# Two FNet and two H3 layers in one kernel: branch loads issued by GpSimd, row statistics on ScalarE, another rotation of PSUM banks

## The chip, the cores and the metric

The kernel runs on one core of a Trainium2 chip. The metric is the device time of one execution in microseconds (us); lower is better. The engines are TensorE (PE: matmuls; PEld: its weight loads), VectorE (DVE), ScalarE (ACT), GpSimd (POOL) and SyncE (SP). ACT, POOL and SP also issue DMAs, each from its own queue, in the order in which its instructions stand.

## The reference

The input x has 2048 rows and 576 columns. Four sublayers are applied, each to the layer norm of what came before, and added to it:

```python
x = x + A(layernorm(x))      # layer 1, Fourier mixing
x = x + B(layernorm(x))      # gated long convolution
x = x + A(layernorm(x))      # layer 2
x = x + B(layernorm(x))
# A(n) = Cr @ (n @ Wr.T) - Ci @ (n @ Wi.T), Cr, Ci: 2048 x 2048, Wr, Wi: 576 x 576
# B(n) = n * y, y = causal_conv(kv, ssm_k) + kv * ssm_D, kv = shift_conv(k) * v
```

`A` is a DFT over the rows and one over the columns, of which the real part is kept. In `B`, k, v and ssm_k are inputs, so that y depends on no layer: it is computed once (here by transforms in place of the FFT) and used by both `B` sublayers as a gate.

## The kernel before

**Numbers.** Products are made at fp32 accuracy from pairs: `split` (L77) writes the rounded high part on ACT (L78) and the rest on DVE (L79), and each product is three matmuls, high by high, high by low, low by high. Rows are held interleaved, 128 partitions of 16 rows j; x[:, j, :] is a tile of 128 x 576.

**Layer 1.** `layer` (L271) runs 128 steps: 4 blocks tb of 512 output rows, in each 2 matrices g (cosine, sine) of 16 steps k. A step loads one 128 x 512 tile of c_mat (`load_c`, L185; SP's queue), splits it, and issues 14 matmuls of 512 columns into four accumulators s0 to s3 and a bank rm. When a block's g is done, `evac_u` (L235) and `evac_r` empty the banks. The product with W (`hidden`, L247) follows in pieces of 27 matmuls of 288 columns that `finish` (L262) puts between the steps. Its result is row xa, stored in DRAM.

**The branch.** `branch` (L316) is a generator that computes y; the loop at L560 advances it along with the steps of layer 1. First transform, up to step 40: for each j, rows of ssm_k and of v with its shifts of k are loaded (`f1_loads`, L343), combined and split on DVE and ACT (`f1_split`, L358), multiplied by f1c, and written to DRAM as t (L387). Middle pass, steps 43 to 96: 64 groups; `mid_split` (L410) loads 288 KB of t (mid<-t) into a ring of three buffers and splits it, `mid_forward` (L417) transforms it, multiplies the spectra of k and v (ACT L424 to L427, DVE L430 to L433), `mid_inverse` (L438) transforms back and stores (copy L444, DMA L445). Last transform, steps 97 to 112: `i2_split` (L464) loads two tiles of 288 KB for each j (mid<-vd) and i2c, `i2_products` (L474) stores y as yb. f1c and i2c are loaded from POOL's queue (`load_fr`, L140), all other loads of the branch from SP's; stores go from ACT's queue.

**Rows of layer 2.** From step 113 on, `get_x1(m)` (L531) makes row m: it loads xa, `gated` (L493) adds the first `B` sublayer, `normed` (L159) normalises for layer 2, and `to_x` (L165) splits into X. `norm_stats` (L149) takes mean and variance on DVE (bn_stats L153 for each half of a row, bn_aggr L154, eps L155) and the reciprocal root on POOL (L156); `normed` scales on ACT (L162) after a small DVE operation (L161). A second function, `normed_x` (L501), serves half of layer 1's rows: sums and squares are taken on ACT with accumulated outputs (L504, L506), small operations on DVE (L505, L507, L509), the power on POOL (L508), the scaling on ACT (L510).

**Layer 2.** Its block 0 runs as 32 ordinary steps. At the same time normalised rows come back from DRAM (`build_load`, L598) and `build` (L607) makes the sums and differences of X ("X's sums") that the next blocks need: from step B_FROM = 18 on, two of the four parts of a `build` in each step, a new `build` every second step. After steps 15 and 31 the accumulators are emptied by `save_u` (L644: ACT L646, then a store) and `store_r` (L649: ACT L652, DVE L653). Blocks 1 to 3 are computed by `strassen` (L720): seven products m in the order 5, 1, 6, 2, 7, 3, 4, each of four steps kp. `load_step` (L668) loads c_mat by 512 KB and sums it on DVE (L671, L677). Each product goes into a pair of banks, s0 and s1 or s2 and s3. Products 2 and 4 accumulate onto products 1 and 7 and use their banks; every other product takes `pair()` (L72), which alternates by a counter at each call. So 5, 1, 6, 7 and 3 take pairs in turn, 2 has 1's and 4 has 7's. After a product ACT or DVE empties its banks (L755 to L780; 2's is ACT L762, 4's DVE L776 and `store_r`). The last stage is `hidden` for all four blocks, with the second `B` sublayer.

**Order.** A scheduler orders each engine's instructions ahead of time from the order in which the program issues them; each engine then runs its own list in order and waits for semaphores. `tc.issue_after` puts an instruction behind a named other one.

The lines that the change and the prediction's steps touch are these; line numbers are those of the profile of the kernel before.

Of the kernel before, what the change touches and what calls it, by code (L numbers as in the profile page):

```python
# [10 lines left out]
F32 = mybir.dt.float32  # L11
# [6 lines left out]
D = 576  # L18
# [23 lines left out]
STAT = 20  # L42
STATIC = 14
B_LOAD = 15
B_FROM = 18
X_RING = 8
CSB = 5
X_END = J * 2 * D
RT_AT = 8 + 4 * STAT
# [5 lines left out]
def fnet_h3_kernel(ctx: ExitStack, tc: tile.TileContext, x, c_mat, w_re, w_im, k_pad, v, shift_k,  # L55
                   ssm_k, ssm_d, f1c, i2c, midc, out):
    nc = tc.nc
# [9 lines left out]
        return psp.tile([P, NT], F32, tag="b", bufs=3, name="bk")  # L67

    acc4 = [psp.tile([P, NT], F32, tag=f"s{i}", name=f"s{i}") for i in range(4)]
    pairs = [0]  # L70

    def pair():  # L72
        pairs[0] += 1
        at = pairs[0] % 2 * 2
        return acc4[at:at + 2]

    def split(h, l, src):  # L77
        nc.scalar.activation(h, src, AF.Copy)  # L78
# [12 lines left out]
    def region_b(dt, name):  # L91
        return sb.tile([P, 6 * WIDE], dt, tag="rb", name=name)
# [9 lines left out]
    ring = {}  # L102
# [28 lines left out]
    lay(flts, 8, ("stat", STAT, 4), ("rt", NT, 1))  # L131
    lay(mats, X_END, ("cs", WIDE, 3))

    anchor, stored, pows = [], [], []

    def load_after(dst, src):
        with tc.issue_after(anchor[-1]):
            return nc.sync.dma_start(dst, src).ins

    def load_fr(dst, src):  # L140
        if pows:
# [17 lines left out]
    def normed(src, y):  # L159
        mv, rs, nb = norm_stats(src)  # L160
        nc.vector.tensor_scalar(nb, mv[:, 0:1], rs, -1.0, op0=OP.mult, op1=OP.mult)  # L161
        nc.scalar.activation(y, src, AF.Identity, bias=nb, scale=rs)  # L162
        return y
# [9 lines left out]
    t_d = [dr.tile([P, J, 2, 2, HD], F32, name=f"t{h}") for h in range(2)]  # L173
# [11 lines left out]
    def load_c(step):  # L185
        g, tb, k = step
        raw = ring["craw"]()
        anchor.append(load_after(raw, c_mat[g, tb, k]) if anchor else nc.sync.dma_start(raw, c_mat[g, tb, k]).ins)
        c = ring["cs"]()
        t = c[:, :NT], c[:, NT:]  # L190
        split(t[0], t[1], raw)
        CT[step] = t
# [123 lines left out]
    def branch():  # L316
# [15 lines left out]

        def load_k(i):
            t = two(ring["k"]())
            nc.sync.dma_start(t, bass.AP(tensor=k_pad.tensor, offset=k_pad.offset + 2 * i * D,
                                         ap=[[J * D, P], [1, 2 * D]]))
            for n in range(2):
                kr[2 * i + n] = t[:, n, :]
# [4 lines left out]
        def f1_loads(j, src):  # L343
            if fcs[0] != j:
                fc = quads(ring["fc"]())
                load_fr(fc, f1c[j])
                fcs[:] = j, fc
            r = ring["land" if src else "v"]()
            nc.sync.dma_start(r, (ssm_k if src else v)[:, j, :])
            if not src:  # L350
                if not wt:
                    load_w4()
                while loaded[0] < min((J + 4) // 2, 2 + j, j // 2 + KR):
                    load_k(loaded[0])
                    loaded[0] += 1
            return r, fcs[1]
# [52 lines left out]

        def mid_split(hf, qg):  # L410
            df = parts("df")
            nc.sync.dma_start(df[1].bitcast(F32),
                              t_d[hf][4 * qg:4 * qg + 4].rearrange("q j c s d -> (q j c) (s d)"))
            split_in(*df)
            return df

# [47 lines left out]
        def i2_split(j):  # L464
            fc = quads(ring["fc"]())
            load_fr(fc, i2c[j])
            vf = []
            for c in range(2):
                vf.append(parts("vf"))
                nc.sync.dma_start(vf[c][1].bitcast(F32), v_d[:, j, c])  # L470
                split_in(*vf[c])
            return fc, vf

# [41 lines left out]
    def load_x(j):  # L515
        if j < J:
            XL[j] = ring["x"]()
            nc.sync.dma_start(XL[j], x[:, j, :])
# [12 lines left out]
    def get_x1(j):  # L531
        if j in ready:
            return
        ready.add(j)
        xa = ring["xa"]()
        nc.sync.dma_start(xa, xa_d[j])
        xb = gated(xa, j)
        nc.sync.dma_start(xb_d[j], xb)
        y = normed(xb, xa)
        stored.append(nc.sync.dma_start(y_d[j // 2][:, j % 2, :], y).ins)  # L540
        X[j] = to_x(y, j)

# [5 lines left out]
    br = branch()  # L548
    wl = load_w()
    load_x(0)  # L550
    load_x(1)
    for used in range(1, K_FIRST + 1):
        next(br)
        if used <= 2:
            load_c((0, 0, used - 1))
        if used == PRE:
            get_x0(0)
        if used == PRE + 1:
            get_x0(1)
    for n in layer(get_x0, lambda j: x[:, j, :], done0, pending):  # L560
        if n <= F1_END:
            want = K_FIRST + (F1_16 * n // 16 if n <= 16 else F1_16 + (32 - K_FIRST - F1_16) * (n - 16) // (F1_END - 16))
        elif n <= MID_END:
            want = 33 + 64 * max(0, n - W_END) // (MID_END - W_END)
        else:
            want = min(114, 97 + 17 * (n - MID_END) // (I2_END - MID_END))
        while used < want:
            next(br, None)
            used += 1
        if F1_END < n <= W_END:  # L570
            for _ in range(3):
                next(wl, 0)
        if n >= W_SAVE and n % 2 == 0:
            next(wl, 0)
        if n > W_END:
            finish(pending, 1)
        m = n - PREP
        if m == 0:
            lay(flts, SC_AT + 3 * NT + 2 * D, ("xa", D, 2), ("yb", D, 2))
            lay(region_b(F32, "gate"), 0, ("xa", D, 3), ("yb", D, 3))  # L580
        if 0 <= m < TB * (TB - 1):
            get_x1(m)
    T, R, t7 = {}, {}, []
# [136 lines left out]
    def strassen():  # L720
        acc, rem = {}, {}
        for n, (tb, m, kp) in enumerate(steps):
            if kp == 0:
                if m in (2, 4):
                    acc[m] = acc[1 if m == 2 else 7]
                else:
                    acc[m] = pair()
                if m in (5, 1):
                    g = REMS[m][0]
                    rem[g] = psp.tile([P, NT], F32, tag="rm", name="rm") if g else bank()  # L730
            for i in range(2):
                ahead(n + 4, 2 * n + i + CSB)
                c = cs.pop(2 * n + i)
                first, last, more = kp == 0 and i == 0, kp == KP - 1 and i == 1, m in (2, 4)
                ch, cl = c[:, 0], c[:, 1]
                for d in range(2):
                    ps = acc[m][d]
                    xh, xl = left(m, kp, i, d)
                    mm(ps, xh, ch, first and not more, False, more)
                    mm(ps, xh, cl, False, False, more)  # L740
                    mm(ps, xl, ch, False, last, more)
                if m in REMS:
                    ps, xr = rem[REMS[m][0]], left_r(m, kp, i)
                    mm(ps, xr, ch, first and not more, False)
                    mm(ps, xr, cl, False, last and more)
            if kp == KP - 1:
                if m == 5:
                    m5 = post("both")
                    for i in range(2):
                        nc.scalar.activation(m5[:, i, :], acc[5][i], AF.Copy)  # L750
                elif m == 1:
                    u2 = post("both")
                    for i in range(2):
                        nc.scalar.activation(u2[:, i, :], acc[1][i], AF.Copy)
                elif m == 6:  # L755
                    for i in range(2):
                        nc.vector.tensor_tensor(u2[:, i, :], u2[:, i, :], acc[6][i], OP.add)
                    nc.vector.tensor_tensor(m5, m5, u2, OP.add)
                elif m == 2:
                    t = post()  # L760
                    for i in range(2):
                        nc.scalar.activation(t[:, i, :], acc[2][i], AF.Copy)  # L762
                    store_u(tb, 0, 0, t)
                    store_r(tb, 0, rem[0])
                elif m == 7:
                    t = post()
                    for i in range(2):
                        nc.vector.tensor_tensor(t[:, i, :], m5[:, i, :], acc[7][i], OP.add)
                    store_u(tb, 1, 1, t)
                elif m == 3:  # L770
                    for i in range(2):
                        nc.vector.tensor_tensor(m5[:, i, :], m5[:, i, :], acc[3][i], OP.add)
                    store_u(tb, 0, 1, m5)
                else:
                    for i in range(2):
                        nc.vector.tensor_tensor(u2[:, i, :], u2[:, i, :], acc[4][i], OP.add)  # L776
                    store_u(tb, 1, 0, u2)
                    store_r(tb, 1, rem[1])
            yield tb, m, kp
# [122 lines left out]
```

## Time and profile before

| what | value |
|---|---|
| median of 3 runs | 1257.11 us (1254.49 to 1259.69) |
| profiled execution | 1256.88 us |
| its span (first to last instruction) | 1254.0 us |
| granted TensorE clock | 0.997 |
| matmuls | 6320 |
| DMA moved | 258.28 MB, mean 206 GB/s |

A page of the profile has the busy time of each engine, the chain of work that ended last, the costliest groups of instructions (line, engine, operation, output and inputs by their names in the program, shape, count; then busy time and mean duration in ns; then the idle time of the engine just before them, with what ended it), and the DMAs by line with the time from issue to landing. Other views of the same trace give the waits of an engine ("PE bk L64 <- ACT f1r L78: 9.8, 1, 9.8": matmuls into bk waited for ACT at L78, in all 9.8 us, once, at most 9.8 us), busy times in stretches of the span, and the instructions in order of time. "bk" are three rotating PSUM banks, "s" the four accumulators, "mats" X and the split c_mat. Idle time of an engine that is not the bottleneck costs nothing.

The stages in the trace: head to about 60 us; first transform of the branch beside layer 1 to about 210; loading of W to 260; middle pass 260 to 570; last transform 570 to 655; rows of layer 2 from 655; layer 2's block 0 ends at about 848; Strassen blocks to 1133; last products with W to 1254.

### The profile page before, as it was taken

How to read it: one execution, taken by the hardware profiler on the slowest of the kernel's cores; microseconds unless marked ns; L12 is line 12 of the kernel's file. 1: busy time of each engine (PE TensorE's matmuls, PEld its weight loads, DVE VectorE, ACT ScalarE, POOL GpSimd, SP SyncE). 2: the span in 40 equal slices, each digit the busy share in tenths (PEclk: the TensorE clock that was granted, in tenths of full speed). 3: DMA queues.
4: the chain of work that ended last, by engine and by line, in shares of the span. 5: the costliest groups of instructions: out<-in, count | busy, mean ns of one | idle time of the engine just before them, and what ended most of it. 6: DMA issues, size and time to landing. Idle time of an engine off the chain costs nothing.

```text
span 1254.0 us, 18238 instructions
## 1 busy us (share of the span) xinstructions
PE 1193.0 (95%) x6320; PEld 1027.0 (82%) x6320; DVE 860.0 (69%) x1591; ACT 631.9 (50%) x1250; POOL 73.8 (6%) x102
## 2 busy tenths in 40 slices
PE   6999999999999999999998899999999999999997
PEld 5788887988789877788886698788778777879997
DVE  7999894478865788863359954765666667675674
ACT  6865665277855788753453422534344344450210
POOL 2210000000000000000013210000000000000111
PEclk9999999999999999999999999999999999999999
DMA  9979887446645645547898844763574577777631
GB/s 311 321 251 296 275 259 229 143 137 181 202 153 178 180 141 161 158 122 241 257 292 279 266 148 162 250 229 106 142 269 135 144 247 249 243 268 224 208 136 48
DMA packets 141646, 258.28 MB, mean 206 GB/s; under 512 B 15345, under 2 KB 39921, under 8 KB 141554
## 3 DMA queue, kind: packets, MB, share of 16 engines
q1 hardware_dynamic: 102674, 205.73, 52.0%
q10 hardware_dynamic: 33984, 42.48, 9.7%
q0 software_dynamic: 4896, 8.92, 2.7%
q8 instruction: 49, 0.80, 0.3%
q14 instruction: 43, 0.35, 0.1%
HBM read 190.42 MB, written 66.65 MB: 205 GB/s over the span
## 4 chain that ended last, share of the span: by engine, by line
PE 68%; DMA 10%; DVE 9%; ACT 8%; issue 3%; POOL 1%; ACTq 0%; SPq 0%; POOLq 0%; DVEq 0%
PE s L64 35%; PE bk L64 27%; PE rm L64 6%; DMA ph<-in_c_mat 3%; DMA flts<-in_c_mat 2%; DVE mats L79 2%; DMA t<-flts 1%; DVE flts L153 1%; POOL flts L156 1%; ACT mats L78 1%; ACT mid L78 1%; DMA mid<-t 1%; ACT flts L444 1%; DVE ph L677 1%; ACT flts L425 1%
## 5 line engine op out<-in xcount | busy, mean ns | idle before, releaser
L64 PE MATMUL s<-mats 128*128 128x512 f32 x2094 | 525.8, 392 | 14.3 <-DVE mats L79 7.9
L64 PEld LDWEIGHTS s<-mats 128*128 128x128 f32 x2094 | 384.6, 188 | 91.6 <-DVE mats L79 10.8
L78 ACT ACTIVATE mats<-flts 128x512 fp32r<-128x512 f32 x209 | 130.8, 626 | 148.2 <-PE rm L64 100.0
L79 DVE TENSOR_TENSOR mats<-flts,mats 128x512 fp32r<-128x512 f32 x209 | 142.6, 684 | 58.6 <-ACT mats L78 58.1
L64 PEld LDWEIGHTS bk<-mid 128*128 128x128 f32 x768 | 111.5, 188 | 34.7 <-ACT flts L444 13.6
L64 PE MATMUL bk<-mid 128*128 128x288 f32 x768 | 127.5, 302 | 12.6 <-ACT flts L444 7.6
L64 PE MATMUL bk<-w,u 128*128 128x288 f32 x864 | 123.0, 296 | 3.2 <-ACT w L78 1.2
L64 PEld LDWEIGHTS bk<-w,u 128*128 128x128 f32 x864 | 118.0, 188 | 7.1 <-ACT w L78 1.6
L79 DVE TENSOR_TENSOR mid<-mid 128x576 fp32r<-128x576 f32 x96 | 72.4, 756 | 57.2 <-ACT mid L78 52.2
L64 PE MATMUL rm<-mats 128*128 128x512 f32 x338 | 105.7, 390 | 1.5 <-DVE flts L432 1.2
L78 ACT ACTIVATE mid<-mid 128x576 fp32r<-128x576 f32 x96 | 65.5, 683 | 72.0 <-DMA mid<-vd 41.7
L156 POOL TENSOR_TENSOR flts<-flts 128x1 f32<-128x1 f32 x56 | 46.8, 837 | 579.7 <-DVE flts L155 576.4
L64 PEld LDWEIGHTS rm<-mats 128*128 128x128 f32 x338 | 63.2, 188 | 15.1 <-DVE flts L432 1.4
L64 PE MATMUL bk<-f1r 128*128 128x288 f32 x384 | 61.7, 305 | 13.8 <-ACT f1r L78 9.8
L64 PEld LDWEIGHTS bk<-f1r 128*128 128x128 f32 x384 | 57.6, 195 | 18.7 <-ACT f1r L78 9.8
L64 PE MATMUL s<-t,mats 128*128 128x512 f32 x258 | 64.4, 389 | 0.0
L386 ACT ACTIVATE flts<-bk 128x288 f32<-128x288 f32 x128 | 47.9, 408 | 24.2 <-DMA t<-flts 13.7
L64 PEld LDWEIGHTS s<-t,mats 128*128 128x128 f32 x258 | 48.7, 189 | 10.2
L64 PE MATMUL bk<-mats 128*128 128x288 f32 (+1 forms) x340 | 56.7, 309 | 0.0
L64 PE MATMUL s<-mats,u 128*128 128x512 f32 x198 | 50.3, 389 | 1.9 <-DVE ph L776 1.9
L78 ACT ACTIVATE mats<-ph 128x512 fp32r<-128x512 f32 x45 | 27.8, 629 | 45.5 <-DVE ph L677 17.5
L64 PEld LDWEIGHTS bk<-mats 128*128 128x128 f32 x340 | 48.8, 188 | 2.0
(141 smaller groups left out, 1553.1 us busy)
## 6 DMA issues: line engine op xcount, KB each, us to landing
flts<-in_c_mat SPq DMA_DIRECT2D x150, 256.0 KB, 3.5
ph<-in_c_mat SPq DMA_DIRECT2D x48, 512.0 KB, 4.1
t<-flts ACTq DMA_DIRECT2D x64, 288.0 KB, 4.5
mid<-t SPq DMA_DIRECT2D x64, 288.0 KB, 3.0
flts<-in_c_mat SPq DMA_DIRECT2D x36, 512.0 KB, 5.1
vd<-flts ACTq DMA_DIRECT2D x64, 144.0 KB, 3.0
mid<-vd SPq DMA_DIRECT2D x32, 288.0 KB, 4.3
ud<-ph ACTq DMA_DIRECT2D x12, 512.0 KB, 5.4
```

What stands on the lines that cost most here:

```text
L64: nc.tensor.matmul(ps, lhsT, rhs, start=first, stop=last, skip_group_check=more)
L78: nc.scalar.activation(h, src, AF.Copy)
L79: nc.vector.tensor_tensor(l, src, h.bitcast(F32), OP.subtract)
L153: nc.vector.bn_stats(st[:, i, :], src[:, i * HD:(i + 1) * HD])
L156: pows.append(nc.gpsimd.tensor_tensor(rs, ve, mhalf, OP.pow).ins)
L386: nc.scalar.activation(so[:, c, :], ps[:, :HD], AF.Copy)
L425: nc.scalar.activation(kk[hi, 0, :], pk[lo, :HD], AF.Copy)
L444: nc.scalar.activation(vo, pv[:, :HD], AF.Copy)
L677: nc.vector.tensor_tensor(src, src, r, OP.add)
```

## The change

Six edits:

- From step 15 of layer 1 on (BULK_FROM), the branch's loads of k, ssm_k, v, t and vd are issued by GpSimd (`load_bulk`), each behind the last POOL power issued; before that step by SyncE, as they were.
- `get_x1` calls `normed_x` in place of `normed`, with buffers of their own ("xj") for the discarded output.
- The rings "xa" and "yb" in the gate region have four buffers in place of three.
- `pair` remembers the last pair used, the shared pair of products 2 and 4 included, and returns the other one. So 7 no longer takes 2's pair, and the next block's 5 no longer 4's.
- B_FROM is 20 in place of 18: X's sums begin two steps of layer 2 later.
- The second load of x is issued after the branch's first step in place of before it.

```diff
-B_FROM = 18
+B_FROM = 20
+BULK_FROM = 15
...
-    pairs = [0]
-    def pair():
-        pairs[0] += 1
-        at = pairs[0] % 2 * 2
-        return acc4[at:at + 2]
+    last_pair = [acc4[2:]]
+    def pair(m, acc):
+        if m in (2, 4):
+            last_pair[0] = acc[1 if m == 2 else 7]
+        else:
+            last_pair[0] = acc4[2:] if last_pair[0][0] is acc4[0] else acc4[:2]
+        return last_pair[0]
...
+    def load_bulk(dst, src):
+        if step[0] < BULK_FROM:
+            nc.sync.dma_start(dst, src)
+        else:
+            with tc.issue_after(pows[-1]):
+                nc.gpsimd.dma_start(dst, src)
...
-            nc.sync.dma_start(t, bass.AP(tensor=k_pad.tensor, ...
+            load_bulk(t, bass.AP(tensor=k_pad.tensor, ...
-            nc.sync.dma_start(r, (ssm_k if src else v)[:, j, :])
+            load_bulk(r, (ssm_k if src else v)[:, j, :])
-            nc.sync.dma_start(df[1].bitcast(F32), t_d[hf]...
+            load_bulk(df[1].bitcast(F32), t_d[hf]...
-                nc.sync.dma_start(vf[c][1].bitcast(F32), v_d[:, j, c])
+                load_bulk(vf[c][1].bitcast(F32), v_d[:, j, c])
...
-        y = normed(xb, xa)
+        y = normed_x(xb, xa, ring["xj"]())
...
-    load_x(1)
     for used in range(1, K_FIRST + 1):
         next(br)
         if used <= 2:
             load_c((0, 0, used - 1))
+        if used == 1:
+            load_x(1)
...
-            lay(region_b(F32, "gate"), 0, ("xa", D, 3), ("yb", D, 3))
+            lay(region_b(F32, "gate"), 0, ("xa", D, 4), ("yb", D, 4), ("xj", D, 2))
...
-                if m in (2, 4):
-                    acc[m] = acc[1 if m == 2 else 7]
-                else:
-                    acc[m] = pair()
+                acc[m] = pair(m, acc)
```

`step[0]` is set to n at the head of layer 1's loop.

More of the change, by code (lines that the diff above doesn't have):

```diff
@@ L132, in fnet_h3_kernel @@
     lay(mats, X_END, ("cs", WIDE, 3))
-    anchor, stored, pows = [], [], []
+    anchor, stored, pows, step = [], [], [], [-1]
     def load_after(dst, src):
@@ L334, in load_k @@
             t = two(ring["k"]())
-            nc.sync.dma_start(t, bass.AP(tensor=k_pad.tensor, offset=k_pad.offset + 2 * i * D,
+            load_bulk(t, bass.AP(tensor=k_pad.tensor, offset=k_pad.offset + 2 * i * D,
                                          ap=[[J * D, P], [1, 2 * D]]))
@@ L411, in mid_split @@
             df = parts("df")
-            nc.sync.dma_start(df[1].bitcast(F32),
-                              t_d[hf][4 * qg:4 * qg + 4].rearrange("q j c s d -> (q j c) (s d)"))
+            load_bulk(df[1].bitcast(F32),
+                      t_d[hf][4 * qg:4 * qg + 4].rearrange("q j c s d -> (q j c) (s d)"))
             split_in(*df)
@@ L560, in fnet_h3_kernel @@
     for n in layer(get_x0, lambda j: x[:, j, :], done0, pending):
+        step[0] = n
         if n <= F1_END:
```

## The prediction

> **What bounds the kernel now.** The page first: TensorE is busy nearly all the time, and the chain that ended last is mostly its own work.
>
> ```profile
> PE 1193.0 (95%) x6320; PEld 1027.0 (82%) x6320; DVE 860.0 (69%) x1591; ACT 631.9 (50%) x1250; POOL 73.8 (6%) x102
> PE 68%; DMA 10%; DVE 9%; ACT 8%; issue 3%; POOL 1%; ACTq 0%; SPq 0%; POOLq 0%; DVEq 0%
> ```
>
> Undelayed matmuls follow each other at 0.227 us (512 columns) and 0.132 us (288 columns) in the timeline: 3440 x 0.227 + 2880 x 0.132 = 1161 us. The change keeps all 6320 matmuls, so only the other 93 us of the 1254.0 us span can shrink: 9.8 before the first matmul, 6.9 after the last, 76 of stalls. The table of stretches says where they are.
>
> ```profile
> core 0: us, PE busy (x) PEld busy (x) DVE busy (x) ACT busy (x) POOL busy (x), PEclk, DMA share, GB/s
> 260.00:570.00 310.00, 295.93 (x1608) 250.81 (x1607) 230.54 (x457) 226.97 (x511) 1.58 (x3) 1.00 0.55 165
> 570.00:655.00 85.00, 84.91 (x500) 76.70 (x499) 35.16 (x54) 40.12 (x80) 6.86 (x13) 1.00 0.83 261
> 655.00:717.00 62.00, 52.09 (x236) 41.65 (x235) 55.18 (x160) 24.96 (x37) 19.26 (x23) 1.00 0.84 276
> 792.00:848.00 56.00, 53.05 (x228) 43.39 (x227) 39.97 (x64) 25.28 (x46) 0.00 (x0) 0.97 0.71 233
> 848.00:1133.00 285.00, 275.97 (x1205) 224.81 (x1205) 191.08 (x258) 126.57 (x209) 0.00 (x0) 1.00 0.62 201
> ```
>
> 260 to 570 is the branch's middle pass (TensorE idle 14.1 us), 570 to 655 its last transform (idle 0.1), 655 to 717 the start of layer 2, where rows are gated and normalised (idle 9.9 of 62, VectorE busy 89%), 792 to 848 the end of layer 2's ordinary block, 848 to 1133 the Strassen blocks. TensorE's waits name the releasers:
>
> ```profile
> PE bk L64 <- ACT f1r L78: 9.8, 1, 9.8
> PE s L64 <- DVE mats L79: 8.2, 7, 2.9
> PE bk L64 <- ACT flts L444: 7.6, 14, 1.4
> PE s L64 <- ACT ph L646: 2.9, 1, 2.9
> PE s L64 <- DVE ph L776: 2.6, 2, 1.9
> ```
>
> **1. Loads issued by GpSimd, from step 15.** 129 loads leave SP for POOL: 6 of k, 14 of ssm_k, 13 of v, 64 mid<-t, 32 mid<-vd. SP's issue takes 0.32 to 0.43 us, POOL's 0.53; neither queue is full, so issue time is worth nothing by itself. What can gain is a load that no longer stands behind a blocked c_mat load, what can lose is a later landing. The middle pass decides, since its 64 groups run on ACT, which waits for the load:
>
> ```profile
> 310.48 0.32 SPq L412 DMA_DIRECT2D mid<-t  x1
> 313.99 0.69 ACT L78 ACTIVATE mid<-mid 128x576 fp32r<-128x576 f32 x1 [1.09 <-DMA mid<-t]
> 316.01 0.66 PE L64 MATMUL bk<-mid 128*128 128x288 f32 x3 [0.82 <-ACT flts L444]
> ```
>
> The load is issued when TensorE has freed its buffer (57 of the 64 issues are released by a matmul, not by SP's other work), so there is nothing to gain: cost at least 0. How much later does POOL's load land? The DMA rows, from issue to landing:
>
> ```profile
> mid<-t SPq DMA_DIRECT2D x27, 288.0 KB, 2.9
> mid<-in_i2c POOLq DMA_DIRECT2D x2, 256.0 KB, 3.5
> mid<-vd SPq DMA_DIRECT2D x26, 288.0 KB, 4.4
> mid<-in_i2c POOLq DMA_DIRECT2D x13, 256.0 KB, 5.5
> ```
>
> The first two are from 420 to 560 us, the others from 570 to 655, where DMA is busy 83%. So 0.6 us later in quiet, 1.1 under load. A group takes 4.39 us; ACT's own work in it is 3.8, so about 0.55 us of delay is absorbed. Not absorbed are the places where two groups meet on ACT and TensorE already waits: of the 14 waits at L444 seven are of 0.4 us or more, and one of the four at ACT mid L78 (1.0 us). Eight places x 0.5 = **+4 us**. The upper end: if every load were 1.23 us late (1.1 and the longer issue), each of the 45 or so groups that run in the regular period would lose 1.23 - 0.55, together +31. I take +4, since the stretch's DMA share (0.55) is that of the quiet row. The Trainium skill ("DMA: Bandwidth & Descriptors", section "Issuing engines are not separate DMA queues") says that issuing from several engines saves only the issuing time; here that speaks against a gain, and no row shows one.
>
> Behind a load that waits on POOL for its buffer stand only further loads (f1c, i2c); layer 1's powers are issued before step 15, the rows' powers after the last mid<-vd.
>
> In the first transform (60 to 210 us) and the last, I take 0. In the last TensorE has no idle time and a row's load has some 2 us of slack before it is used. In the first VectorE (busy 83%) and DMA (0.85) set the pace together, and freed SP slots and later landings oppose: -3 to +3.
>
> **2. Second statistics of a layer-2 row on ACT.** In 655 to 717 the chain goes row after row through VectorE's statistics and POOL's power; VectorE is the bound. The groups by form:
>
> ```profile
> L153 DVE BATCH_NORM_STATS2 flts<-flts 128x6 f32<-128x288 f32 x44 | 18.8, 449 | 7.9 <-DMA flts<-xa 7.4
> L154 DVE BATCH_NORM_AGGREGATE flts<-flts 128x2 f32<-128x12 f32 x56 | 11.0, 200 | 0.8
> L161 DVE TENSOR_SCALAR flts<-flts 128x1 f32<-128x1 f32 x24 | 5.1, 213 | 9.6 <-POOL flts L156 9.6
> L506 ACT ACTIVATE early<-early,flts 128x576 f32<-128x576 f32 x8 | 6.2, 774 | 1.8 <-DVE flts L505 1.8
> ```
>
> Per row VectorE loses 2 x 0.449 + 0.200 + 0.144 (L155) + 0.213 = 1.455 us and gets L505, L507 and L509 (0.145 + 0.145 + 0.157 = 0.447): -1.0. ACT gets L504 and L506 with their accumulator reads: 0.679 + 0.194 + 0.774 + 0.193 = 1.84. About 12 rows fall into the stretch: VectorE 55 - 12 = 43, ACT 25 + 22 = 47, TensorE 52. TensorE is then the longest, so the gain ends at its idle 9.9 us. Against it: a row's chain now changes engines ACT, VectorE, ACT, VectorE, POOL, VectorE, ACT, and c_mat's split (ACT L78) queues behind a row's two passes on ACT; TensorE waits for that split. And the same bytes in less time: the DMA share rises from 0.84 to 0.84 x 62/54 = 0.96, so DMA could be next. I take three quarters: **-7.5** (0 to -9.9). The deeper rings of gate (4) are what lets rows overlap. The last four rows are hidden: they end some 8 us before use.
>
> **3. X's sums start at step 20, not 18.** At 792.35 TensorE waits 3.11 us in step 16: ACT's first sum waits 5.28 us for its load, and the evacuation L646, which frees TensorE's bank, stands behind it. In the changed order the evacuation is ahead of the first sum. The sums then end by step 28 of 32, under a TensorE without waits: **-2.8** (-3.1 to 0).
>
> **4. Alternating banks.** In every Strassen block product 7 followed product 2 on the same banks, and the next block's 5 followed 4. The waits: 1.2 and 1.1 (2 to 7, ACT L762), 0.85 and 2.06 (4 to 5, DVE L776), 0.46: 5.7 us. But at 2 to 7 the chain runs through c_mat's loads and VectorE's sum L677, not through the bank, and 10 us later TensorE waits there anyway:
>
> ```profile
> 914.30 0.74 PE L64 MATMUL s<-mats,t 128*128 128x512 f32 x2 [0.83 <-ACT mats L78]
> ```
>
> TensorE that starts 7 earlier waits longer here: 0. At 4 to 5 the next product also needs bank rm after 12 matmuls, which L653 frees behind L776 and a 1.22 us L671: about half a microsecond at each is left. **-1.0** (-5.7 to 0).
>
> **5. One x load behind the first branch step.** The first matmul waits for ssm_k, which is issued one SP issue (0.43) earlier: **-0.4** (-1 to +0.5).
>
> **Sum:** -0.4 + 4 - 7.5 - 2.8 - 1.0 = -7.7. The profiled execution took 1256.88 us (span 1254.0 and 2.9 around it), 0.2 below the median of the three runs: 1256.9 - 7.7 = **1249.2**.
>
> **Rivals.**
> - *Rows bound by hand-offs or DMA:* part 2 gains only 1.5 us. For it: the share of 0.96, and ACT's double role. Against: ACT idles 37 us of 62 today. 1256.9 - 0.4 + 4 - 1.5 - 2.8 - 1.0 = 1255.2, the same.
> - *Late loads decide (slower):* each mid<-t lands over 0.55 us later than SP's. At the loaded rows' 1.1: 45 x 0.55 = +24.8 in place of +4, 1270.0. For it: ACT waits for the load already in 28 groups (24.8 us); against: the quiet rows' 0.6.
> - *Descriptors starved:* if POOL's descriptors could not be written while VectorE works, loads would be up to 2.5 us late: (2.5 - 0.55) x 45 = +88, about 1340. Against it: POOL's issues take 0.53 us also where VectorE is busy 83%, and VectorE's 128x576 subtraction takes 0.755 us with and without one beside it. By the Trainium skill ("SBUF — State Buffer", section "SBUF: two separate sides") a VectorE operation in its two-port mode locks GpSimd out of writing descriptors; these rows do not show it.
> - *All covers hold:* loads 0, rows -9.9, sums -2.8, banks -3, start -0.4: 1240.8.
>
> **Chances.** A run of this kernel tells 0.5% (6.3 us; 1250.8 to 1263.4) from no change. Forecast 0.47, itself 1244 to 1253 (0.36 faster, 0.11 same); hand-offs 0.18 (same); late loads 0.20 (slower); starved 0.03 (slower); all covers 0.12 (faster). Faster 0.48, same 0.29, slower 0.23. The range goes from all covers to the middle of late loads.
>
> **What the profile after would show.** Right: a row stretch of some 54 us with VectorE near 43 and ACT near 47; no wait on the evacuation in step 16; no wait of a product's first matmul on L762's or L776's successors, but a longer one of the kind at 914.30; first matmul at 9.4; ACT's wait for mid<-t up from 24.8 to about 40 and TensorE's on the copy of L444 to about 12. Wrong: a middle pass longer by 20 us or more (late loads), or a row stretch that keeps 60 us with VectorE idle (hand-offs, DMA).

## The result and the profile after

The changed kernel takes 1266.9 us (median of 6 runs, 1263.17 to 1268.99), the kernel before beside it 1257.92 us: a ratio of 1.0071, 95% interval 1.0045 to 1.0097. It is slower by 0.7%. The forecast was 1249.2 and faster. The profiled execution took 1263.17 us, the fastest of the six, with a span of 1261.4.

The first view is the page of the changed kernel: busy times, then the chain that ended last.

```profile
PE 1200.6 (95%) x6320; PEld 1029.4 (82%) x6320; DVE 849.1 (67%) x1559; ACT 655.9 (52%) x1314; POOL 146.4 (12%) x231
PE 50%; issue 15%; DMA 13%; DVE 11%; ACT 7%; POOL 3%; SPq 0%; POOLq 0%; ACTq 0%; DVEq 0%
```

The same 6320 matmuls, 11 us less on VectorE and 24 more on ScalarE, close to the 12 and 22 worked out. But TensorE's own part of the chain falls from 68 to 50%, while "issue" (time in which the engine waited for nothing that the profile shows) rises from 3 to 15% and DMA from 10 to 13%. TensorE's waits in the changed kernel (engine and line waited for; total, times, longest) follow. Line numbers are those of each run's own kernel: the matmul stands at L64 to L66, ScalarE's split at L78 to L83, VectorE's at L79 to L84.

```profile
PE bk L65 <- ACT f1r L82: 6.5, 1, 6.5
PE bk L65 <- ACT flts L455: 6.2, 7, 1.1
...
PE bk L65 <- ACT u L82: 4.3, 1, 4.3
...
PE s L65 <- ACT mats L82: 3.9, 4, 1.6
...
PE bk L65 <- DVE f1r L83: 3.3, 1, 3.3
```

The waits on the evacuation of step 16 (L646 before) and on the copies that free product banks (L762, L776 before) are gone; the wait for VectorE's part of c_mat's split (8.2 before, DVE L83 now) is down to 2.0. New are one wait of 4.3 for ACT u and one of 3.3 at the start. These sums are not larger than before, so the loss is not in a few long waits; TensorE's busy time is 7.6 us longer for the same matmuls. Fixed stretches of the span no longer hold the same work (it is up to 18 us late), so the table below counts by work: the time from the start of the n-th matmul to that of a later one, from each trace's own profiled execution. The start column is from the span's start to matmul 150. All kernels issue their matmuls in nearly the same order.

| kernel | median us | ratio to before (95%) | start | first transform 150-600 | 600-1050 | middle 1050-2850 | last 2850-3450 | rows 3450-3750 | step 16 3900-4050 | Strassen 4050-5400 |
|---|---|---|---|---|---|---|---|---|---|---|
| before | 1257.9 | | 45.1 | 91.5 | 88.3 | 335.9 | 106.8 | 70.9 | 38.3 | 318.1 |
| changed | 1266.9 | 1.0071 (1.0045-1.0097) | 46.1 | 96.0 | 88.5 | 346.5 | 108.0 | 68.3 | 33.5 | 313.9 |
| bulk_only | 1276.3 | 1.0160 (1.0136-1.0184) | 44.7 | 99.4 | 87.4 | 345.9 | 108.0 | 71.2 | 38.4 | 318.3 |
| bulk_f1 | 1263.9 | 1.0065 (1.0041-1.0089) | 44.9 | 98.1 | 87.8 | 337.6 | 110.4 | 71.7 | 37.6 | 318.6 |
| bulk_18 | 1273.7 | 1.0172 (1.0141-1.0203) | 44.7 | 93.1 | 89.8 | 348.7 | 111.0 | 70.4 | 35.8 | 320.2 |
| bulk_late | 1264.2 | 1.0099 (1.0071-1.0126) | 44.8 | 91.6 | 88.4 | 345.0 | 108.6 | 69.2 | 37.4 | 316.5 |
| no_bulk | 1246.3 | 0.9920 (0.9897-0.9942) | 46.2 | 92.5 | 90.1 | 337.1 | 107.6 | 67.7 | 33.5 | 312.1 |
| no_bulk_x | 1242.3 | 0.9915 (0.9892-0.9938) | 45.8 | 91.0 | 87.5 | 336.1 | 108.8 | 67.5 | 33.5 | 312.9 |
| rows_only | 1255.3 | 0.9983 (0.9963-1.0003) | 44.9 | 91.9 | 88.1 | 336.5 | 109.1 | 68.9 | 38.6 | 316.2 |
| rows8 | 1241.2 | 0.9911 (0.9886-0.9936) | 46.2 | 90.9 | 86.9 | 336.4 | 106.4 | 64.6 | 33.5 | 312.2 |
| pairs_only | 1251.8 | 0.9966 (0.9949-0.9983) | 45.0 | 91.5 | 86.4 | 337.3 | 108.1 | 71.2 | 37.8 | 313.5 |
| sums_only | 1252.7 | 0.9973 (0.9956-0.9990) | 44.5 | 91.4 | 87.9 | 335.8 | 108.6 | 71.5 | 33.5 | 318.5 |
| late_t2 | 1248.1 | 0.9962 (0.9947-0.9977) | 44.5 | 92.1 | 86.2 | 327.7 | 108.9 | 70.4 | 40.5 | 317.1 |
| sp_split_late | 1259.4 | 1.0048 (1.0026-1.0071) | 44.8 | 92.1 | 85.8 | 339.8 | 111.5 | 70.9 | 35.5 | 315.7 |
| pool_split_late | 1263.3 | 1.0087 (1.0058-1.0116) | 44.8 | 91.3 | 89.2 | 338.6 | 112.7 | 70.4 | 34.9 | 316.8 |
| best | 1249.8 | 0.9974 (0.9955-0.9994) | 44.7 | 92.4 | 87.2 | 339.8 | 110.6 | 68.5 | 33.5 | 313.1 |
| best2 | 1236.6 | 0.9845 (0.9818-0.9871) | 44.6 | 91.4 | 88.5 | 330.9 | 108.3 | 66.3 | 34.3 | 313.7 |

The level moves by a few us from one set of runs to another (the kernel before had medians of 1251.7 to 1257.9 beside these), so totals are compared by the ratio column. Stages that an edit does not touch differ between traces by about 2 us in the first transform and the middle pass, by 2.5 in the rows, and by 4 to 6 in the others; a smaller difference in one stage says nothing.

Part of these differences is TensorE's granted clock. In each of the seventeen traces it falls to a half, for 3.41 us (at times 6.83), one to six times before the last matmul. By estimate 3.41 us at half the clock cost 1.7 us. In all 44 cases the fall begins between 1.8 us before and 1.5 us after the end of a TensorE wait of 1.1 us or more; many waits of that length have none behind them.

Changed against before, by stage: start +1.0, first transform +4.5, middle +10.6, last +1.2, rows -2.6, step 16 -4.8, Strassen -4.2, and +1.5 behind the last matmul; 7.3 of the 7.4 us by which the span grew. The middle pass is where the time went. ScalarE's longest wait there, and the loads of t, in the changed kernel from 260 to 570 us:

```profile
ACT mid L82 <- DMA mid<-t: 37.1, 26, 4.1
```

```profile
mid<-t POOLq DMA_DIRECT2D x59, 288.0 KB, 3.3
```

Before it was 24.8 us in 28 waits.

### The profile page after: what moved, and what is told of

Its sections match the earlier page's. It is cut to its first block, busy times and chain, and to the rows that moved or that the text cites. A ratio compares the mean times of both kernels' runs of the same rounds, so it can differ in the third digit from the quotient of the medians.

```text
span 1261.4 us, 18277 instructions
## 1 busy us (share of the span) xinstructions
PE 1200.6 (95%) x6320; PEld 1029.4 (82%) x6320; DVE 849.1 (67%) x1559; ACT 655.9 (52%) x1314; POOL 146.4 (12%) x231
## 4 chain that ended last, share of the span: by engine, by line
PE 50%; issue 15%; DMA 13%; DVE 11%; ACT 7%; POOL 3%; SPq 0%; POOLq 0%; ACTq 0%; DVEq 0%
PE s L65 26%; PE bk L65 19%; PE rm L65 4%; DMA ph<-in_c_mat 3%; DMA mid<-t 3%; DMA t<-flts 2%; DMA mid<-vd 2%; DVE mats L83 2%; POOL mid L149 1%; DMA flts<-in_c_mat 1%; ACT mats L82 1%; ACT mid L82 1%; DMA f1f<-in_ssm_k 1%; POOL flts L519 1%; DVE ph L690 1%
## 5 line engine op out<-in xcount | busy, mean ns | idle before, releaser
L83 DVE TENSOR_TENSOR mats<-flts,mats 128x512 fp32r<-128x512 f32 x209 | 142.8, 686 | 49.6 <-ACT mats L82 47.2
L65 PE MATMUL bk<-mid 128*128 128x288 f32 x768 | 135.3, 306 | 17.1 <-ACT flts L455 6.2
L65 PEld LDWEIGHTS bk<-w,u 128*128 128x128 f32 x864 | 120.7, 192 | 10.7 <-ACT u L82 5.0
L83 DVE TENSOR_TENSOR mid<-mid 128x576 fp32r<-128x576 f32 x96 | 72.6, 756 | 74.9 <-ACT mid L82 70.3
L167 POOL TENSOR_TENSOR flts<-flts 128x1 f32<-128x1 f32 x40 | 39.0, 975 | 538.9 <-DVE flts L166 534.9
L149 POOL DMA_DIRECT2D mid<-t x64 | 34.4, 538 | 331.2 <-PE bk L65 220.3
L65 PEld LDWEIGHTS s<-t,mats 128*128 128x128 f32 x258 | 48.4, 188 | 10.1
```

Source lines behind the costliest of these rows:

```text
L65: nc.tensor.matmul(ps, lhsT, rhs, start=first, stop=last, skip_group_check=more)
L83: nc.vector.tensor_tensor(l, src, h.bitcast(F32), OP.subtract)
L149: nc.gpsimd.dma_start(dst, src)
L167: pows.append(nc.gpsimd.tensor_tensor(rs, ve, mhalf, OP.pow).ins)
```

## The experiments

Unless said otherwise an experiment is the kernel before with only the edit named.

**bulk_only: only the loads on GpSimd.**

```diff
-            nc.sync.dma_start(...)       # k, ssm_k, v, t, vd
+            load_bulk(...)               # BULK_FROM = 15
```

> The kernel before with the loads moved to GpSimd as the only edit. Theory (late loads): the loss is the moved loads' own, +5 us in the first transform and +10 us in the middle pass, so about 1272, the middle pass (matmuls 1050 to 2850 of the program) 347 us or more against 336. Rival (the sum of small things): the loads alone cost the +4 of the forecast, about 1261, and the rest of the loss comes with the other edits.

Measured 1.0160: about 20 us. The theory holds, the small-things rival falls: this edit costs more than the whole change.

**no_bulk: the changed kernel, all loads on SyncE** (`BULK_FROM = 1000`).

> The changed kernel with every load of the branch on SyncE again. Theory (late loads): first transform and middle pass as long as before, the other gains stay, about 1250 (1257.5 - 2.5 rows - 3 evacuation - 4 banks + 1 start + noise). Rival (other edits): it stays above 1257.

Measured 0.9920, 10 us faster than before and some 19 faster than the changed kernel; the middle pass is back at 337.1. The theory holds: the other edits gain 10.1 us, more than this run was expected to show and a little less than the 11.7 that the prediction's parts 2 to 5 add up to.

**pairs_only: alternating banks.** The edit is `pair` as in the change.

> The kernel before with alternating bank pairs as the only edit. The forecast's working: -1.0, since c_mat's loads and L653 replace the waits for banks. The trace of the changed kernel suggests -4: the four waits for banks go and the waits that were to grow grow less. 1256.5 by the first, 1253.5 by the second.

Measured 0.9966 (4.3 us, 2.1 to 6.4), and 4.6 us in the Strassen blocks, which take 312.1 to 313.9 us in the seven kernels with this edit and 315.7 to 320.2 in the ten without. TensorE's waits there, from 848 to 1133 us, in this kernel:

```profile
PE s L65 <- ACT mats L82: 4.1, 4, 1.8
...
```

The waits on L762 and L776 (2.0 and 2.6 before) are gone, and the wait that was to take their place, for c_mat's split on ACT, went from 3.7 to 4.1. No wait for bank rm appears.

**rows_only: second statistics on ScalarE, rings of four.**

> The kernel before with the second statistics of layer-2 rows on ScalarE (and the rings of four) as the only edit. The forecast's working: -7.5, 1250. What the changed kernel showed: -2.5 between matmuls 3450 and 3750, 1255. If the row stage loses again 4 us where ScalarE's evacuation of the last layer-1 block stands behind rows (a wait of bk on ACT u), the second is right and does not come from the moved loads.

Measured 0.9983 (0.9963 to 1.0003): unclear in the total, 2.0 us in the stage. The table of stretches shows the work moved as worked out for ScalarE:

```profile
655.00:717.00 62.00, 54.95 (x252) 44.88 (x252) 50.85 (x148) 45.46 (x92) 20.40 (x24) 0.98 0.89 292
```

ACT is busy 45 us (25 before; 47 forecast), TensorE 55 (52); VectorE, at 51 us, is above the 43 forecast. The rest of the gain is lost at one place. The timeline of this kernel, TensorE's and ScalarE's instructions in order:

```profile
710.03 0.61 PE L65 MATMUL rm<-mats 128*128 128x512 f32 x2
...
712.63 0.67 ACT L177 ACTIVATE mats<-gate 128x576 fp32r<-128x576 f32 x1
713.76 0.87 ACT L520 ACTIVATE gate<-gate,flts 128x576 f32<-128x576 f32 x1 [0.47 <-DVE flts L519]
714.66 0.68 ACT L177 ACTIVATE mats<-gate 128x576 fp32r<-128x576 f32 x1
715.25 2.04 ACT L81 ACTIVATE u<-s 128x512 fp32r<-128x512 f32 x4
715.89 2.53 PE L65 MATMUL bk<-w,u 128*128 128x288 f32 x9 [5.24 <-ACT u L81]
```

At 710.6 TensorE has finished layer 1's last step and needs its accumulators emptied (u<-s). ScalarE's list has two rows' passes ahead of that; the rows wait on VectorE in between, and TensorE stands for 5.2 us. Its granted clock is at a half for 6.8 us from 714.5 on, by estimate another 3.4 us; no such fall lies in this stage of the kernel before.

**rows8: no_bulk, with rows 8 to 11 on VectorE as before.**

```diff
-        y = normed_x(xb, xa, ring["xj"]())
+        y = normed(xb, xa) if j in ROWS_DVE else normed_x(xb, xa, ring["xj"]())
```

> The changed kernel with all the branch's loads on SyncE, and rows 8 to 11 of layer 2 with their second statistics on VectorE as before (the other twelve on ScalarE). Theory: the row stage's gain was lost where the evacuation of layer 1's last accumulators stands on ScalarE behind the passes of two rows (a wait of bk on ACT u of 4.4 to 5.4 us). In this kernel's order the evacuation stands directly behind the last split; the wait should shrink to 1 us or less and the time to about 1243. Rival: hand-offs or DMA bind the rows, and the wait comes back elsewhere, 1246 or more.

TensorE's waits from 640 to 740 us, in this kernel:

```profile
PE s L66 <- DVE flts L167: 2.5, 2, 2.2
PE s L66 <- DVE flts L517: 0.7, 1, 0.7
```

The wait on ACT u is gone (4.3 in no_bulk), 2.2 us came back on VectorE, and the row stage takes 64.6 us in place of 67.7. By the trace the theory holds here. But best and best2 below, which treat the rows alike, again have one wait for VectorE at this place, of 3.6 and 3.5 us, as the rival has it. The totals (0.9911 and 0.9920, from two sets of runs) do not separate.

**no_bulk_x: no_bulk, x's second load in its old place.**

> The changed kernel with all the branch's loads on SyncE and the second x load in its old place. The trace showed the first matmul 3.3 us earlier and a wait of 3.3 us for VectorE right behind it, where the second row's statistics stand ahead of the split's low part. If so, the later load loses about 1 us over the first 150 matmuls, and this kernel is 1 us faster than the one with the later load: 1245. Rival: the later load gains its 0.4, 1246.7.

0.9915 against 0.9920 and a start of 45.8 against 46.2: no difference that these runs can tell. What the later load does is plain in the changed kernel's timeline:

```profile
6.52 1.09 PE L65 MATMUL bk<-f1r 128*128 128x288 f32 x3 [6.52 <-ACT f1r L82]
8.98 0.82 DVE L164 BATCH_NORM_STATS2 flts<-early 128x6 f32<-128x288 f32 x2 [3.38 <-DMA early<-in_x]
...
10.15 0.75 DVE L83 TENSOR_TENSOR f1r<-f1f,f1r 128x576 fp32r<-128x576 f32 x1
...
10.95 1.33 PE L65 MATMUL bk<-f1r 128*128 128x288 f32 x4 [3.34 <-DVE f1r L83]
```

The first matmul comes 3.3 us earlier, three are done, and the fourth waits 3.3 us for the split's low part: that stands on VectorE behind the second row's statistics, which wait 3.4 us for the x load now issued later. The wait moved from one engine to another.

**sums_only: B_FROM = 20.**

> The kernel before with X's sums from step 20 on as the only edit. The forecast's working: -2.8 (the wait of 3.1 us at step 16). In the stage table of the changed kernel matmuls 3900 to 4050 took 33.5 us in place of 38.3: -4.8, of which 33.5 is close to the nominal spacing. 1250 at the level of the last runs (1253.8) by either; the stage decides: 33.5 means that all waits there came from the early sums, 35 that the banks' rotation took some.

0.9973 (3.4 us, 1.3 to 5.5); the stage is 33.5 us, as in the changed kernel, so its wait came from the early sums. That wait was 2.9 us, but the stage is 4.8 us shorter. The rest is the clock: in the kernel before, the twelve matmuls behind the wait take 4.58 us, where the twelve ahead of it take 2.88.

```profile
789.18 2.88 PE L64 MATMUL s<-mats 128*128 128x512 f32 x12
795.46 4.58 PE L64 MATMUL s<-mats 128*128 128x512 f32 x12 [2.95 <-ACT ph L646]
```

From 796.6 us the granted clock is at a half for 3.4 us. Of the ten kernels with B_FROM = 18, the seven with the longer waits here (2.1 to 4.4 us) have such a fall in this stage (37.4 to 40.5 us), the three with the shorter ones (1.1 to 2.0) have none (34.9 to 35.8).

**bulk_late: only the loads from step 41 on (t and vd) on GpSimd** (`BULK_FROM = 41`).

> The kernel before with GpSimd issuing only the loads after step 41: t in the middle pass and vd in the last transform; the first transform's loads stay on SyncE. If the two stages lose by themselves, as the traces of the two kernels with all loads moved show (middle +10, last +1, first +4 to +8), this one is about 1257 + 11 = 1268 and its first transform is as long as before. Rival: the first transform sets the branch behind and the middle pass only inherits it; then nearly nothing is lost here, 1259.

1.0099: the middle pass loses 9.1 us by itself, with a first transform as before. The rival (inherited) falls.

**bulk_f1: only the first transform's loads on GpSimd.**

> The kernel before with GpSimd issuing only the first transform's loads (k, ssm_k, v) from step 15 on; t and vd stay on SyncE. If the two losses add, this costs what all loads cost less what the later loads alone cost, 1.6% - 1.0% = 0.6%, about 7 us: 1261 at the level of the last runs, all of it in matmuls 150 to 600. Rival: the start of the burst only shifts the branch within layer 1, whose middle pass catches up, and the total grows by under 3 us.

1.0065, and the two losses, 0.65% and 0.99%, add up to the 1.60% of all loads within the intervals. The stage loses 6.6 us, and the total keeps it (the profiled execution is the slowest of its six, 6.2 us above their median, so its later stages are not read here). How it starts is seen where steps reach 15. The table of stretches for 70 to 80 us, first of bulk_late (SyncE here), then of bulk_only:

```profile
70.00:80.00 10.00, 9.90 (x47) 7.77 (x46) 9.97 (x17) 6.83 (x13) 0.00 (x0) 1.00 0.90 314
```

```profile
70.00:80.00 10.00, 6.94 (x26) 5.34 (x25) 7.86 (x14) 5.02 (x10) 2.95 (x6) 0.85 1.03 358
```

VectorE and TensorE are nearly without a pause in the first; in the second VectorE is idle 2.1 of 10 us, TensorE 3.1. The loads of bulk_only from 64 to 82 us (KB each, us from issue to landing):

```profile
f1f<-in_k_pad POOLq DMA_DIRECT2D x4, 576.0 KB, 9.2
flts<-in_c_mat SPq DMA_DIRECT2D x4, 256.0 KB, 6.5
f1f<-in_ssm_k POOLq DMA_DIRECT2D x3, 288.0 KB, 6.1
flts<-in_v POOLq DMA_DIRECT2D x3, 288.0 KB, 6.9
```

The loads stand behind GpSimd's last power, which ends at 65.4 us, and then go out in a burst with f1c's (nine from 65.4 to 69.7 us); c_mat on SyncE lands in 6.5 us among them (3.6 in bulk_late, 4.1 in the kernel before).

**bulk_18: all loads on GpSimd, from step 18** (`BULK_FROM = 18`).

> All loads on GpSimd as in the run with only that edit, but from step 18 on in place of 15, when GpSimd's last powers of layer 1 are done. Theory (start): from step 15 the loads stand behind the last power and then go out ten at once at 65 to 70 us, with 9 us to land and VectorE idle; from step 18 that is milder, the first transform (matmuls 150 to 600) takes 93 to 95 us in place of 99, and the total about 1270. Rival (GpSimd's queue all along: loads that wait for VectorE hold up those behind them): 98 or more, 1275.

Inconclusive. The stage is 93.1 as the start theory says, but the total is 1.0172, not better than from step 15: this trace has 2 to 3 us more in each of three later stages, at a granted clock of 0.989 in place of 0.993. Nor is the burst milder: GpSimd's first loads stand behind the same power and go out as eight from 65.4 to 69.7 us, and c_mat lands in 6.4 us from 64 to 82 us, yet the stage loses 1.6 us where bulk_only loses 7.9. So the burst alone does not explain the first transform's loss; what else does stays open.

**late_t2: t's load from SyncE in three issues.**

```diff
-            nc.sync.dma_start(df[1].bitcast(F32), src)
+            for lo, hi in ((0, 1), (1, 2), (2, P)):
+                nc.sync.dma_start(df[1].bitcast(F32)[lo:hi], src[lo:hi])
```

> The kernel before, all loads on SyncE, but each 288 KB load of t in three issues: one row, one row, 126 rows. The bytes are the same; the large piece is issued about 0.65 us later, as late as GpSimd's load lands after the release (0.27 later issue and 0.4 longer landing, from the traces). Theory (lateness, whatever issues it): the middle pass grows by about 10 us, 1267. Rival (something of GpSimd's own, such as its descriptors or the order that the scheduler writes for it): by under 3 us, 1259.

Both expectations were wrong: the middle pass became 8.2 us shorter, the total 0.9962. ScalarE's waits in it, 260 to 570 us:

```profile
ACT mid L81 <- DVE flts L444: 23.9, 29, 2.1
...
ACT mid L81 <- DMA mid<-t: 3.1, 5, 0.9
```

The wait for the load fell from 24.8 to 3.1 us, with a load that is issued in 0.87 us instead of 0.32. The order of ScalarE's list had changed with the edit. Counted in the traces, in the kernel before 39 of the 64 splits of t stand ahead of the copies of the spectra of both groups before their own, and all of ScalarE's waiting for t is at these; 24 stand behind the copies of one of the two. In this kernel 12 and 49 do. With GpSimd's loads in the scheduler's order (the changed kernel) the counts are 39 and 23, almost as before, and of 40.5 us of waiting for t in the whole trace 38.8 are at the 39. So the load's lateness shows where its split stands early, and hardly elsewhere.

So a new theory: lateness costs what it costs because of the place of the split in ScalarE's list.

**sp_split_late and pool_split_late: the split held behind the group's last copy, loads on SyncE and on GpSimd.**

```diff
-            split_in(*df)
+            with tc.issue_after(kk_end[-1]) if kk_end else ExitStack():
+                nc.scalar.activation(df[0], df[1].bitcast(F32), AF.Copy)
+            nc.vector.tensor_tensor(df[1], df[1].bitcast(F32), df[0].bitcast(F32), OP.subtract)
```

`kk_end` holds the last copy (L427 before) of each group.

> The kernel before, loads on SyncE, with ScalarE's split of a middle-pass load held behind the last copy of the spectra (L427) of the group ahead of it; nothing else. New theory: what costs time is not the load's lateness but the place of its split in ScalarE's order: the scheduler puts it so early that ScalarE waits for the load with everything behind it. With the split late, ScalarE hardly waits, and the middle pass (matmuls 1050 to 2850) takes about 328 us in place of 336: 1249. Rival: the three issues gained by themselves, and this order gains nothing, 1257.

> The same order of ScalarE as in the run beside it, but the loads after step 41 issued by GpSimd. Theory (place of the split): the load has some 2 us of slack, so GpSimd's 0.67 us later landing costs nothing in the middle pass: 328 to 330 us there, total within 3 us of its neighbour. Rival (lateness counts by itself, or GpSimd's descriptors do): again about 9 us more than the neighbour, 1258.

ScalarE's list in the middle pass is the same in both. Loads of t, 260 to 555 us, first from SyncE, then from GpSimd:

```profile
mid<-t SPq DMA_DIRECT2D x58, 288.0 KB, 2.8
```

```profile
mid<-t POOLq DMA_DIRECT2D x59, 288.0 KB, 3.5
```

They land 0.7 us later from GpSimd, and from matmul 1200 to 2850 both kernels take 316.9 us (314.2 before, 323.4 with GpSimd's loads and the scheduler's order in bulk_late). In neither does ScalarE wait for t. So in this stretch the later landing, and anything else that GpSimd does to these loads, costs nothing where the split leaves it room: here the theory of the pair holds. The gain that was expected of the late split did not come, 339.8 in place of 328: TensorE now waits 22 times some 0.2 us for the split itself. A split held late in every group is too late in many; the three-issue load moved it only in some. The last transform loses another 4.7 us: TensorE waits 3.0 us at its head for ScalarE's first split there, and 3.4 us at half the granted clock follow. The totals of the two differ by 3.9 us, more than the 3 that were expected at most; the intervals overlap. In their traces the last transform has 1.2 of it, and 3.4 lie between matmuls 600 and 1050. There GpSimd issues its first three loads of t at once, from 209.3 us, and TensorE waits once 3.3 us for the split of W (1.0 us at most in the neighbour), with 3.4 us at half clock behind it. Four of the five kernels with t on GpSimd have a wait of 2.6 to 3.3 us for W there, all others at most 1.6. That the loads cause it is likely, but not shown.

**best: all gains, split held late.**

> All that has gained so far: alternating banks, sums from step 20, second statistics on ScalarE for all rows but 8 to 11, rings of four, loads on SyncE, x's second load in its old place, ScalarE's split of the middle pass late. If the gains add: 1241 (rows 8 to 11 on VectorE) - 1 (x's load) - 8 (split) = 1232 by the level of these runs.

0.9974, 1249.8 us in place of 1232: against rows8 (0.9911) a loss of 8 us where the split was to gain 8. The two traces differ by 12.4 us: 3.4 in the middle pass and 4.2 in the last transform, as in the pair above, and 3.9 in the rows, where TensorE waits 3.6 us once for VectorE.

**best2: all gains, three-issue load.** no_bulk_x, rows 8 to 11 as in rows8, t's load as in late_t2.

> Alternating banks, sums from step 20, second statistics on ScalarE for all rows but 8 to 11, rings of four, all branch loads on SyncE, x's second load in its old place, and t's load in three issues (1, 1 and 126 rows), which moves ScalarE's split later in the scheduler's order only where there is room. If the gains add: 0.9911 (rows 8 to 11) less 1 us less the three issues' 0.4%, about 1235 at the level of the last runs; with the split held late by hand it was 1250.

0.9845 (0.9818 to 0.9871), 1236.6 us, as expected: 20 us faster than the kernel before and the fastest here.

## Why the prediction was wrong

**Part 1, loads on GpSimd: forecast +4, measured about +20.** Three steps of it failed.
- "0.55 us of delay is absorbed", with 0.5 to 0.6 of delay. The delay was taken from issue to landing. But GpSimd also issues later after the matmul that frees the buffer: the load starts 0.46 us (median) behind the start of that matmul in the changed kernel, 0.19 before, and lands 3.5 us (mean) after the issue in place of 3.1. That is 0.67, past the point that the forecast itself named. Its two terms, which it took one or the other, add up to 45 x (0.67 - 0.55) + 8 x 0.67 = 5.4 + 5.4 = 10.8; measured 9.1 to 12.8 in the four traces with these loads on GpSimd and the scheduler's order. (Of the 14 waits eight, not seven, are of 0.4 us or more; this changes little.) That late loads cost time through ScalarE was right, the size of the delay was not.
- What the cover is made of was not asked. It is the place of one instruction in ScalarE's list: with the split behind the copies the same 0.7 us cost nothing (316.9 and 316.9). The forecast's own sign shows how little was covered: ScalarE's wait for t was to grow by 15 us and the time by 4; it grew by 12.3, and the middle pass by 10.6. TensorE's wait on the copy did not go to 12 us but to 6.2 (7.6 before). The time is in matmuls that stand further apart: before the 768 matmuls bk<-mid the page has 17.1 us idle in place of 12.6, and for them 135.3 us busy in place of 127.5.
- In the first transform "I take 0" (-3 to +3). Measured +4.5 to +7.9 in the stage from step 15 on (+1.6 from step 18) and 0.65% in the total of bulk_f1. The forecast let freed SyncE slots and later landings oppose, and held that layer 1's powers are issued before step 15. But the last power ends at 65.4 us (66.0 in the changed kernel), the loads stood behind it, and then nine went out within 4.3 us (eight within 3.8 in the changed kernel), where SyncE had spread them between c_mat's loads. This is what the traces show where the loss begins; that it is the whole cause is not shown, since bulk_18 has nearly the same burst. The upper bound of 31 in the text was for the middle pass alone.

The rival "late loads decide" named the sign, the point from which it decides (0.55 us) and nearly the time (1270.0). The nearness is in part luck: it put 24.8 us into the middle pass, where 10.6 were, and nothing into the first transform. The rival of starved descriptors is not seen: in the pair above VectorE works beside GpSimd's loads through the whole middle pass, and the two take the same time from matmul 1200 to 2850; the 2.5 us that it worked with stand on no row. The Trainium skill ("DMA: Bandwidth & Descriptors", section "Issuing engines are not separate DMA queues") says that issuing from several engines only saves the issuing time. No run here shows another gain; that it can cost, the runs show (0.99% in bulk_late).

**Part 2, rows: forecast -7.5, measured -2.0 to -3.4 in the stage.** TensorE's waits for VectorE went, as forecast (from 640 to 740 us 7.9 and 2.0 before, 0.7 and 1.1 in rows_only). The text did name what queues behind the passes on ScalarE, c_mat's split, but not the evacuation of layer 1's last accumulators, which TensorE needs at just that time: 4.2 to 5.2 us, with 3.4 to 6.8 us at half the granted clock behind. With that out of the way the stage gains 6.3 (rows8), 4.6 (best2) and 2.4 (best); in the last two a wait for VectorE has taken its place. DMA's share did rise, to 0.91 in rows8, and the stage still became shorter; 0.96 was not tried.

**Part 3, sums: forecast -2.8, measured -4.8 in the stage and -3.4 (1.3 to 5.5) in the total.** Right in what it is; the size lacked the 3.4 us at half the granted clock that followed the wait.

**Part 4, banks: forecast -1.0, measured -4.3 (2.1 to 6.4).** The step that failed is "TensorE that starts 7 earlier waits longer here: 0". It waited 4.1 in place of 3.7 us in all. The chain's view had led through c_mat's load at 2 to 7; that the chain passes by a wait does not mean that the wait comes back in full. That the loads, issued when a buffer is free, came earlier too was not measured. The half microsecond for bank rm did not come either.

**Part 5, x's load: forecast -0.4, measured between 0 and +1** (start of 46.1 to 46.2 us in the three kernels with it, 44.5 to 45.8 in the others). The first matmul did come earlier, by more than forecast, but VectorE's order turned it into a wait behind it. The forecast looked at one engine's wait only.

The edits alone give +1.60% - 0.17% - 0.34% - 0.27% = +0.82%, with the start's 0 to 1 us; the change measured +0.71% (0.45 to 0.97). That parts 2 to 5 together came near their forecast (-10.1 in no_bulk, forecast -11.7) is luck: part 2 gave less than half of its 7.5 us, parts 3 and 4 more than theirs.

## What to carry to other kernels

Where each engine runs a list that a scheduler has fixed, the price of a later load is set by where its first user stands in that list: ask for the slack there, from the release of the buffer to the use, and count the issuing engine's delay before the issue as well as the landing after it. When work is moved to an engine with much idle time, look for the one instruction of that engine that the bound engine needs soon, and see what now stands ahead of it. A load put behind a named instruction of another engine waits until that instruction has run, whenever the program issued it: look in the trace when it runs. And a wait of the bound engine can cost more than its length: look at the granted clock behind it.

## What the runs showed of the hardware

A load of 288 KB issued by GpSimd landed 0.3 to 0.7 us later after its issue than the same one from SyncE (3.3 against 3.0, 3.5 against 2.8 us), and started 0.27 us later behind the event that released it. Nine loads went out within 4.3 us; by kind the loads of that time took 6 to 10 us (median) to land, with a DMA share of 1.03 in the stretch, and c_mat's loads among them took 6.5 in place of 3.6 us. In that stretch TensorE stood 3.1 us and then ran 3.4 us at half the granted clock, which makes the mean of 0.85.

The falls of the granted clock to a half came in lengths of 3.41 and 6.83 us, all 44 of them beside a TensorE wait of 1.1 us or more. One wait of 2.9 us with such a fall behind it cost 4.8 us in its stage.
